# Uneven steps for the row maxima, and a new place for half a division, in a routed-attention and MLP kernel

## The chip, the cores and the metric

The kernel runs on one core of a Trainium2 chip. The metric is the device time of one execution in microseconds. Before the change it is 959.33 us, the median of three runs (959.2 to 959.88).

## What is computed

Two blocks in a row. The first is attention with routing: every query and key of a head goes to the nearest of 16 centroids, and a query sees only keys with its own centroid. The second is an MLP with its own activation.

```python
q_assign = np.argmax(einsum('bhsd,hcd->bhsc', q_n, c_n), axis=-1)   # k_assign likewise
mask = q_assign[:, :, :, None] == k_assign[:, :, None, :]
scores = np.where(mask, scale * q @ k.T, -1e9)
scores = scores - np.max(scores, axis=-1, keepdims=True)
attn = np.exp(scores); attn /= attn.sum(-1, keepdims=True) + 1e-9
x = (attn @ v) laid out as (B*S, H*D)
h = x @ w_in; g = h * erf(softplus(h)); out = g @ w_out
```

B = 4, H = 8, S = 768 keys, D = 64; the MLP has 3072 tokens, 512 and 2048 wide. All in float32.

## The kernel before

**Pairs and periods.** Two heads make a pair; there are 16 pairs. A pair has 12 units: two halves of 384 queries by six blocks of 128 keys. `period(p, i)` (from line 1345) does two units, u and u + 1, and there are six periods, i = 0 to 5, in a pair. All calls to the engines are recorded in program order (`InOrder`, line 130), so the order in which `period` calls its helpers is the order in each engine's queue. That is why every line of the profile is L138; instructions are told apart by the tiles that they write and read.

**TensorE in a period.** In this order: the first maxima step (`step_ahead`, lines 1332 and 1360); the score products of two units (`products`, f32, `sc<-qT,kT` or `sc<-more_out`); the first half of the second maxima step; the routing mask and shift of unit u (`scores`, bf16, `sc<-qm,km`), the second half of the maxima step, and `scores` of u + 1; then for the two units of the period before the product of the exponentials with v (`attend`, `turned<-pr,in_v`). After a half is complete (i = 0 and 3), `divide` (line 575) makes the denominators on TensorE (`turned<-more_out,minus`) in one bank `turned`, while the products for that half stand in the other.

**Row maxima** (`maxima_step`, line 463). The softmax's shift is made ahead, in bf16, for the pair half a pair later. For each of six blocks t of 128 queries, two steps cover the 768 keys, 384 each. A step has two passes for each of the two heads: products with the bf16 copies (`wide<-kv,qv`) and, on top, the mask (`wide<-km,qm`). VectorE then reduces both heads' 384 columns to one maximum for a row (`nmx<-wide`, 128 x 768 elements in all). `wide` is one tile of two banks of 512 columns, so no step can begin before the reduce of the one before has read it. Step number i of `maxima_step` gives t and half by `divmod(i, 2)`; in period i of a pair t = (i + 3) mod 6, the first step of the period is half 0 and the second is half 1. The second is called with `behind=True`: its mask pass uses only rows 32 to 63 and 96 to 127 of the array, and stands between the two `scores`, which use rows 0 to 31 and 64 to 95. In the first step the mask pass uses all rows and stands alone. After three blocks of t a small reduce makes `lowest`, which `turn` (line 494) brings into rows at the start of periods 0 and 3.

**Routing** (`choose`, line 407), for the pair after the next: VectorE transposes the similarities (`sims<-turned`), takes each token's maximum over 16 centroids (here written into spare columns of a score bank, `sc<-sims`), compares (`hot<-sims,sc`), and transposes twice (`aside`, `hotT`). It is a generator; `next(routing[0])` in `period` places one operation after the other. `masks` (line 437) multiplies the result by a matrix of picks (`turned<-hotT,pick`), at the places in a period that the table `MASKS` (line 50) gives: (period, place) to tensor and half. The place 0 is ahead of the products, 1 behind them, 2 behind the second `scores`. A mask above place 1 uses 32 rows for a head (`narrow`), at place 0 or 1 it uses 64.

**Division** (`divide`), a generator as well: after ScalarE's `inv`, VectorE makes `den`, divides the two halves of the products in place (`turned<-turned,inv`, twice), and writes their product with `den` to `more_out`, from where four DMAs on SP's queue store it to `x_dram`. It runs in the period after it was created, so in periods 1 and 4.

**Weights.** Beside this, the MLP's weights are loaded and brought into another form by ScalarE (`size`, `rest`, `sign`), VectorE (`bounded`, `shifted`: two tensor_scalars on 128 x 512) and GpSimd (`summed`), one block in periods 3 and 4 and one over 3, 5, 0 and 1 (lines 1400 to 1437). GpSimd also adds up the exponentials (`accumulate`).

The tail of `period` that fixes VectorE's order around the change, lines 1413 to 1418:

```python
        if i == 3:
            next(routing[0], None)
            if early(n1):
                shifted(n1)
            for _ in range(2):
                next(routing[0], None)
```

Of the kernel before, what the change touches and what calls it, by code (L numbers as in the profile page):

```python
# [14 lines left out]
ALU = mybir.AluOpType  # L15
ACT = mybir.ActivationFunctionType
AX = mybir.AxisListType
PSUM = bass.MemoryType.PSUM

P = 128  # L20
B, H, S, D = 4, 8, 768, 64
# [4 lines left out]
HW = S // 2  # L26
QW = HW // 2
TW = QW + 1
HJ = NJ // 2
HP = H // 2  # L30
NPAIR = B * HP
DM, DFF = H * D, 2048
NFT = DFF // P
# [13 lines left out]
N_LATE = 4  # L47
PLACE_OF = [n % 5 for n in range(25)] + [2, 3, 2]
LAST_X = 11
MASKS = {(0, 2): ("k", 0), (2, 0): ("q", 0), (2, 2): ("k", 1), (5, 2): ("q", 1)}  # L50
FIRST_MASKS = {(2, 0): ("k", 0), (2, 1): ("q", 0), (2, 2): ("k", 1), (5, 2): ("q", 1)}

KAPPA = {1: (0, 1), 2: (0, 0), 0: (1, 1), 3: (1, 0)}
# [93 lines left out]
def kernel(  # L147
# [24 lines left out]
    turned = [ps.tile([P, 512], F32, name=f"turned{i}") for i in range(2)]  # L172
# [149 lines left out]
    def bounded(n):  # L322
        w = w_steps[n][0]
        ve.tensor_scalar(out=w, in0=w, scalar1=2.0, scalar2=None, op0=ALU.max)
# [5 lines left out]
    def shifted(n):  # L330
        w = w_steps[n][0].bitcast(U32)
        ve.tensor_scalar(out=w, in0=w, scalar1=3, scalar2=None, op0=ALU.logical_shift_left)
# [130 lines left out]
    def maxima_step(p, i, sm=wide, behind=False):  # L463

        st = pairs[p]
        nmx = maxima[p % 2]
        t, half = divmod(i, 2)

        def passes(a, b, start, rows):
            for e in range(2):  # L470
                r = slice(e * D + rows.start, e * D + rows.stop)
                te.matmul(
                    sm[:, e, 0:HW], lhsT=st[a][r, t * P : (t + 1) * P],
                    rhs=st[b][r, half * HW : (half + 1) * HW], start=start, stop=not start,
                )

        passes("qv", "kv", True, slice(0, D))
        if behind:
            yield
        passes("qm", "km", False, slice(Q, D) if behind else slice(0, D))  # L480
        if behind:
            yield
        ve.tensor_reduce(
            out=nmx[:, :, t, half], in_=sm[:, :, 0:HW], axis=AX.X, op=ALU.max, negate=True
        )
        if i in (NJ - 1, 2 * NJ - 1):
            h = i // NJ
            ve.tensor_reduce(
                out=lowest[h][:, :, ::D].rearrange("p t e -> p e t"),
                in_=nmx[:, :, h * HJ : (h + 1) * HJ], axis=AX.X, op=ALU.min,  # L490
            )
            turns.append((p, h))
# [21 lines left out]
    def products(u):  # L514
        p, half, j = units[u]
        if u in sc_of:
            return
        st = pairs[p]
        sc = sc_of[u] = ps_s.tile([P, 2, 512], F32, name="sc", tag="s")
        for e in range(2):  # L520
            r = slice(e * D, (e + 1) * D)
            te.matmul(
                sc[:, e, 0:HW], lhsT=st["kT"][r, j * P : (j + 1) * P],
                rhs=st["qT"][r, half * HW : (half + 1) * HW], start=True, stop=False,
            )
# [49 lines left out]
    def divide(u):  # L575

        p, half, _ = units[u]
        st = pairs[p]
        av = st["av", half]

        psum = turned[1 - half][:, 0:QW]
        for g in range(4):
            te.matmul(psum[g * Q : (g + 1) * Q], lhsT=minus, rhs=st["acc", half][:, g], start=True, stop=True)

        if u + 1 < len(units):
            inv = routep.tile([P, QW], F32, name="inv")
            den = routep.tile([P, QW], F32, name="den")
        else:
            inv, den = part_of(0, 4 * HW, QW), part_of(1, 0, QW)
        ae.activation(out=inv, in_=psum, func=ACT.Ln, bias=alleps, scale=-1.0)  # L590
        ae.activation(out=inv, in_=inv, func=ACT.Exp, scale=-1.0)
        yield
        ve.scalar_tensor_tensor(
            out=den, in0=psum, scalar=S * EPS, in1=inv, op0=ALU.subtract, op1=ALU.mult
        )
        for k in range(2):
            raw = av[:, k, 0:QW]
            ve.scalar_tensor_tensor(
                out=raw, in0=raw, scalar=av[:, k, QW : QW + 1], in1=inv, op0=ALU.add, op1=ALU.mult
            )  # L600
        yield
        x = part_of(0, (2 * p + half) % 4 * HW, HW).rearrange("p (k x) -> p k x", k=2)
        ve.scalar_tensor_tensor(
            out=x, in0=den.unsqueeze(1).to_broadcast([P, 2, QW]), scalar=2.0, in1=av[:, :, 0:QW],
            op0=ALU.add, op1=ALU.mult,
        )
        b, r = divmod(p, HP)
        for g in range(4):
            rows_of, at = r * P + g // 2 * D, b * S + half * HW + g % 2 * QW
            nc.sync.dma_start(  # L610
                out=x_dram[rows_of : rows_of + D, at : at + QW].rearrange("(k r) x -> r k x", k=2),
                in_=x[g * Q : (g + 1) * Q],
            )
        if half == 1:
            del pairs[p]
        yield
# [728 lines left out]
    def period(p, i):  # L1345
        u = 2 * NJ * p + 2 * i
        n1, n2 = 2 * p - 1, 2 * p
        early = lambda n: 0 <= n < N_EARLY

        def mask(place):  # L1350
            which = (MASKS if p else FIRST_MASKS).get((i, place))
            if which:
                return masks(p + 1, *which, turned[0 if i in (0, 5) else 1], place > 1, ve if i == 0 else ae)
            return lambda: None

        if u > 0:
            for which in turns if i in (0, 3) else ():
                turn(*which)
                turns.remove(which)
            step_ahead(u)  # L1360
        mask(0)()
        next(part[0], None)
        if i == 5:
            next(routing[0], None)
        if i == 0 and p:
            run(routing[0])
        if u == 2:
            next(routing[0])
        products(u)
        products(u + 1)  # L1370
        mask(1)()
        second = step_ahead(u + 1, True) if u > 0 else iter(())
        next(second, None)
        rows = D if u == 0 or u + NJ >= len(units) else Q
        scores(u, rows)
        next(second, None)
        if i:
            next(second, None)
        next(part[0], None)
        scores(u + 1, rows)  # L1380
        later = mask(2)
        if i == 0:
            later()
            later = lambda: None
            next(second, None)
        if i == 3:
            similarities(p + 2)
            routing[0] = choose(p + 2, sc_of[u + 1][:, 0], True)
        curve(u)
        later()  # L1390
        curve(u + 1)
        if u == 0:
            step_ahead(1)
            similarities(1)
            routing[0] = choose(1, turned[0])
            next(routing[0])
            next(routing[0])
            vectors(1, "q")
            vectors(1, "k")
        if i == 0 and early(n1 - 1):  # L1400
            bounded(n1 - 1)
            shifted(n1 - 1)
            sign(n1 - 1)
        elif i == 1 and early(n1):
            size_and_rest(n1)
        elif i == 3 and early(n1):
            bounded(n1)
            sign(n1)
        elif i == 5 and early(n2):
            rest(n2)  # L1410
        for _ in range(min(len(forms), FORMS.get(p, {}).get(i, 0))):
            forms.pop(0)[0]()
        if i == 3:
            next(routing[0], None)
            if early(n1):
                shifted(n1)
            for _ in range(2):
                next(routing[0], None)
        elif i == 1:
            load(p + 1, "v", v, vp)  # L1420
            if p == 0:
                run(routing[0])
                transposes(2, "q")
        elif i == 2:
            transposes(p + 2, "k")
        elif i == 4:
            vectors(p + 2, "k")
            vectors(p + 2, "q")
        elif i == 5:
            transposes(p + 3, "q")  # L1430
        if u > 0:
            if i in POOL_FORMS.get(p, ()) and forms:
                forms.pop(0)[1]()
            if i == 1 and early(n1 - 1):
                summed(n1 - 1)
            elif i == 4 and early(n1):
                summed(n1)
            for w in (u - 2, u - 1):
                accumulate(w)
            for w in (u - 2, u - 1):  # L1440
                attend(w)
            if i % HJ == 0:
                part[0] = divide(u - 1)
                next(part[0])
        if i == 3 and early(n2):
            size(n2)
# [206 lines left out]
```

## Time and profile before

| | us |
|---|---|
| median of 3 runs | 959.33 |
| the profiled execution | 959.94 |
| its span, first to last instruction | 958.1 |
| maxima steps in the trace, first to last reduce | 12.9 to 396.1 |

| engine | share of the span busy |
|---|---|
| TensorE, matmuls | 99% |
| TensorE, weight loads | 76% |
| VectorE | 83% |
| ScalarE | 56% |
| GpSimd | 56% |

A row of the timeline gives the start, the time from the first start to the last end, engine, line, operation, output and inputs, shape, and how many instructions are merged in it; in brackets stands how long the engine sat idle before, and who ended that. Matmuls overlap: the recorded duration of one is longer than the time until the next can start, so it is the differences of starts that tell what one costs. f32 matmuls are recorded twice each. Two row-tiled matmuls, one for each head, start 3 ns apart and run side by side.

### The profile page before, as it was taken

How to read it: one execution, taken by the hardware profiler on the slowest of the kernel's cores; microseconds unless marked ns; L12 is line 12 of the kernel's file. 1: busy time of each engine (PE TensorE's matmuls, PEld its weight loads, DVE VectorE, ACT ScalarE, POOL GpSimd, SP SyncE). 2: the span in 40 equal slices, each digit the busy share in tenths (PEclk: the TensorE clock that was granted, in tenths of full speed). 3: DMA queues.
4: the chain of work that ended last, by engine and by line, in shares of the span. 5: the costliest groups of instructions: out<-in, count | busy, mean ns of one | idle time of the engine just before them, and what ended most of it. 6: DMA issues, size and time to landing. Idle time of an engine off the chain costs nothing.

```text
span 958.1 us, 22447 instructions
## 1 busy us (share of the span) xinstructions
PE 950.1 (99%) x8954; PEld 728.2 (76%) x8954; DVE 798.0 (83%) x1395; ACT 539.0 (56%) x815; POOL 538.7 (56%) x375
## 2 busy tenths in 40 slices
PE   8999999999999999999999999999999999999998
PEld 3555555555555555588888888998999899989987
DVE  8888888888888887787689889788868987897887
ACT  3777777777777777542524531654257236625541
POOL 1688888778888888897669910360054016202600
PEclk9999999999999999999999999999999999999999
DMA  9345545544454522041403454463445336343533
GB/s 224 61 112 112 112 111 112 112 112 111 90 117 84 132 56 56 22 152 55 177 1 154 154 164 138 135 202 110 155 125 174 115 128 210 110 149 119 157 115 110
DMA packets 172313, 116.06 MB, mean 121 GB/s; under 512 B 131376, under 2 KB 141104, under 8 KB 172208
## 3 DMA queue, kind: packets, MB, share of 16 engines
q1 hardware_dynamic: 169280, 113.41, 42.3%
q8 instruction: 71, 1.16, 0.5%
q10 hardware_dynamic: 2928, 1.21, 0.4%
q14 instruction: 34, 0.28, 0.1%
HBM read 90.21 MB, written 24.38 MB: 120 GB/s over the span
## 4 chain that ended last, share of the span: by engine, by line
PE 95%; DVE 2%; ACT 1%; DMA 1%; issue 0%; DVEq 0%; SPq 0%; ACTq 0%
PE bank L138 41%; PE turned L138 32%; PE sc L138 17%; PE wide L138 6%; DVE nmx L138 1%; DMA out_dram<-osb 0%; ACT a_s L138 0%; DVE osb L138 0%; ACT L138 0%; DVE g L138 0%; DMA in_q<-in_q_dram 0%; DVE g_more L138 0%; DVE kT L138 0%; DVE sims L138 0%; DVE qT L138 0%
## 5 line engine op out<-in xcount | busy, mean ns | idle before, releaser
L138 POOL TENSOR_TENSOR more_out<-more_out,pr 128x768 f32<-128x768 f32 x128 | 217.3, 1698 | 16.2 <-ACT pr L138 6.7
L138 DVE TENSOR_REDUCE nmx<-wide 128x2 f32<-128x768 f32 x189 | 180.5, 955 | 46.4 <-PE wide L138 45.9
L138 ACT ACTIVATE pr<-sc 128x768 f32<-128x768 f32 x192 | 148.7, 810 | 87.2 <-PE wide L138 68.6
L138 POOL TENSOR_TENSOR g<-g 128x512 f32<-128x512 f32 x36 | 47.2, 1310 | 216.6 <-DVE g L138 214.7
L138 PE MATMUL turned<-pr,in_v 128*32 128x193 f32 x3072 | 144.8, 330 | 0.0
L138 PEld LDWEIGHTS turned<-pr,in_v 128*32 128x32 f32 x3072 | 91.5, 109 | 50.7 <-issue 21.3
L138 PE MATMUL sc<-qT,kT 64*128 64x384 f32 x528 | 98.3, 486 | 0.0
L138 DVE TENSOR_TENSOR g<-g 128x512 f32<-128x512 f32 x114 | 79.0, 693 | 15.2 <-PE bank L138 11.7
L138 DVE TENSOR_TENSOR g<-a_s,g 128x512 f32<-128x512 f32 x80 | 73.5, 944 | 5.6 <-ACT a_s L138 5.6
L138 DVE TENSOR_TENSOR g<-bank,g 128x256 f32<-128x256 f32 (+1 forms) x129 | 63.8, 522 | 15.3 <-PE bank L138 8.1
L138 PE MATMUL bank<-w_out,g 128*128 128x256 f32 x328 | 75.4, 379 | 0.0
L138 ACT ACTIVATE a_s<-g 128x1024 f32<-128x1024 f32 (+1 forms) x36 | 41.0, 1149 | 55.9 <-POOL g L138 45.3
L138 PE MATMUL bank<-g_more,g 128*128 128x256 f32 x304 | 71.8, 379 | 0.0
L138 PE MATMUL bank<-x_own,w_in 128*128 128x128 f32 (+1 forms) x432 | 71.6, 308 | 0.0
L138 POOL TENSOR_TENSOR more_out<-pr,pr 128x768 f32<-128x768 f32 x32 | 58.9, 1839 | 20.1 <-ACT pr L138 20.1
L138 PEld LDWEIGHTS bank<-w_out,g 128*128 128x128 f32 x328 | 62.3, 190 | 8.5
L138 PEld LDWEIGHTS <-qv 64*128 64x128 bf16 x384 | 26.9, 93 | 53.4 <-issue 37.3
L138 PEld LDWEIGHTS sc<-qT,kT 64*128 64x128 f32 x528 | 49.2, 187 | 21.9 <-ACT inv L138 3.1
L138 ACT ACT_TABLE_LOAD x40 | 51.3, 1283 | 24.4 <-DVE g L138 23.7
L138 PE MATMUL wide<-kv,qv 64*128 64x384 bf16 x378 | 63.9, 328 | 1.1 <-ACT km L138 0.6
L138 PEld LDWEIGHTS bank<-x_own,w_in 128*128 128x128 f32 x432 | 61.1, 191 | 4.0 <-issue 0.6
L138 PEld LDWEIGHTS bank<-g_more,g 128*128 128x128 f32 x304 | 57.8, 190 | 7.9
(242 smaller groups left out, 2065.3 us busy)
## 6 DMA issues: line engine op xcount, KB each, us to landing
g_more<-b_dram SPq DMA_DIRECT2D x48, 512.0 KB, 3.5
g_more<-w_dram SPq DMA_DIRECT2D x84, 256.0 KB, 2.8
x_own<-in_moe_w_in_dram SPq DMA_DIRECT2D x13, 512.0 KB, 5.4
in_v<-in_v_dram SPq DMA_DIRECT2D x32, 192.0 KB, 3.3
x_dram<-more_out SPq DMA_DIRECT2D x128, 48.0 KB, 1.7
x_own<-x_dram SPq DMA_DIRECT2D x6, 1024.0 KB, 5.4
in_k<-in_k_dram SPq DMA_DIRECT2D x59, 96.0 KB, 2.7
in_q<-in_q_dram SPq DMA_DIRECT2D x58, 96.0 KB, 4.9
```

The source lines that it names most:

```text
L138: ins = getattr(self.engine, name)(*args, **kw)
```

## The change

The split of the 768 keys between the two steps now depends on the block t: 256 + 512 for t = 0, 1 and 4, 352 + 416 for t = 2 and 5, 384 + 384 for t = 3. In VectorE's queue, `hot` moves from the end of period 3 behind the first reduce of period 4; `bounded` moves behind the transpose of the similarities; of the division only `den` and the first half stay ahead of the second reduce of the period, the second half and the product go behind it. The maxima over the centroids are written to spare columns of `turned[0]` in place of a score bank. One mask in period 2 moves from ahead of the products to a new place 3, between the products of u and of u + 1, still 64 rows wide.

```diff
+KEYS = (256, 256, 352, 384, 256, 352)
...
-MASKS = {(0, 2): ("k", 0), (2, 0): ("q", 0), (2, 2): ("k", 1), (5, 2): ("q", 1)}
+MASKS = {(0, 2): ("k", 0), (2, 3): ("q", 0), (2, 2): ("k", 1), (5, 2): ("q", 1)}
...
         t, half = divmod(i, 2)
+        first = KEYS[t]
+        keys = (slice(0, first), slice(first, S))[half]
+        n = keys.stop - keys.start
...
-                    sm[:, e, 0:HW], lhsT=st[a][r, t * P : (t + 1) * P],
-                    rhs=st[b][r, half * HW : (half + 1) * HW], start=start, stop=not start,
+                    sm[:, e, 0:n], lhsT=st[a][r, t * P : (t + 1) * P],
+                    rhs=st[b][r, keys], start=start, stop=not start,
...
-            out=nmx[:, :, t, half], in_=sm[:, :, 0:HW], axis=AX.X, op=ALU.max, negate=True
+            out=nmx[:, :, t, half], in_=sm[:, :, 0:n], axis=AX.X, op=ALU.max, negate=True
...
             ve.scalar_tensor_tensor(
                 out=raw, in0=raw, scalar=av[:, k, QW : QW + 1], in1=inv, op0=ALU.add, op1=ALU.mult
             )
-        yield
+            if k == 0:
+                yield
...
-                return masks(p + 1, *which, turned[0 if i in (0, 5) else 1], place > 1, ve if i == 0 else ae)
+                return masks(p + 1, *which, turned[0 if i in (0, 5) else 1], place == 2, ve if i == 0 else ae)
...
         mask(0)()
+        if i == 4:
+            next(routing[0], None)
         next(part[0], None)
...
         products(u)
+        mask(3)()
         products(u + 1)
...
         if i:
             next(second, None)
-        next(part[0], None)
+            next(part[0], None)
         scores(u + 1, rows)
...
             next(second, None)
+            next(part[0], None)
         if i == 3:
             similarities(p + 2)
-            routing[0] = choose(p + 2, sc_of[u + 1][:, 0], True)
+            routing[0] = choose(p + 2, turned[0], True)
...
         elif i == 3 and early(n1):
-            bounded(n1)
             sign(n1)
...
             next(routing[0], None)
             if early(n1):
+                bounded(n1)
                 shifted(n1)
-            for _ in range(2):
-                next(routing[0], None)
...
                 attend(w)
+            if i == 3:
+                next(routing[0], None)
             if i % HJ == 0:
                 part[0] = divide(u - 1)
```

In the build VectorE's rows from period 3 to 5 then stand as: `sims`, `bounded`, `shifted`, the maxima (`turned<-sims`), first reduce, `hot`, `den`, first half of the division, second reduce, second half, product. Before they are: `bounded`, `sims`, `shifted`, the maxima (`sc<-sims`), `hot`, first reduce, `den`, both halves, second reduce, product.

## The prediction

> **What bounds the kernel now.** I read the page's first lines, then a window over the stretch that the change touches.
>
> ```profile
> span 958.1 us, 22447 instructions
> PE 950.1 (99%) x8954; PEld 728.2 (76%) x8954; DVE 798.0 (83%) x1395; ACT 539.0 (56%) x815; POOL 538.7 (56%) x375
> ...
> 24.00:396.00 372.00, 371.94 (x5356) 212.10 (x5359) 313.66 (x504) 284.98 (x462) 305.77 (x188) 1.00 0.43 97
> ```
>
> The third line covers the time in which row maxima are made (columns: window, length, busy of PE, PEld, DVE, ACT, POOL, granted clock, DMA share). TensorE is busy for all of it at full clock, so only what shortens TensorE's own row of starts counts. But "busy" is a sum of modelled durations that overlap; a small wait hides in it. So next I read the timeline for the starts alone: first the tail of a period i = 3 and the whole of i = 4 on TensorE.
>
> ```profile
> 201.94 1.45 PE L138 MATMUL sc<-qT,kT 64*128 64x384 f32 x8
> 203.23 0.33 PE L138 MATMUL wide<-kv,qv 64*128 64x384 bf16 x2
> 203.49 0.34 PE L138 MATMUL sc<-qm,km 32*128 32x384 bf16 x2
> 203.50 0.34 PE L138 MATMUL wide<-km,qm 32*128 32x384 bf16 x2
> 203.66 0.32 PE L138 MATMUL sc<-qm,km 32*128 32x384 bf16 x2
> ...
> 205.89 0.51 PE L138 MATMUL turned<-more_out,minus 128*32 128x192 f32 x8
> 206.34 0.34 PE L138 MATMUL wide<-kv,qv 64*128 64x384 bf16 x2
> 206.51 0.33 PE L138 MATMUL wide<-km,qm 64*128 64x384 bf16 x2
> 206.67 1.48 PE L138 MATMUL sc<-qT,kT 64*128 64x384 f32 x8
> 208.01 0.34 PE L138 MATMUL wide<-kv,qv 64*128 64x384 bf16 x2
> 208.28 0.34 PE L138 MATMUL sc<-qm,km 32*128 32x384 bf16 x2
> 208.29 0.33 PE L138 MATMUL wide<-km,qm 32*128 32x384 bf16 x2
> ...
> 210.16 0.34 PE L138 MATMUL wide<-kv,qv 64*128 64x384 bf16 x2
> ```
>
> A period has two maxima steps. The first (206.34, 206.51) runs alone: each 384-column pass holds TensorE for 0.16 to 0.17 us. The second has its qv pass alone (203.23) and its qm pass (203.50) between the two score passes (203.49, 203.66), on rows that these leave free, so that one costs TensorE nothing.
>
> The block of score products takes 1.29 us where nothing disturbs it (201.94 to 203.23), but 1.34 in period 4 (206.67 to 208.01), and the pass behind it 0.27 instead of 0.26. That is a wait of 0.06 us. Who causes it stands in VectorE's rows of the same time:
>
> ```profile
> 203.93 0.96 DVE L138 TENSOR_REDUCE nmx<-wide 128x2 f32<-128x768 f32 x1 [0.83 <-PE wide L138]
> 204.81 0.43 DVE L138 TENSOR_SCALAR w_in<-w_in 128x512 f32<-128x512 f32 x1
> 205.16 0.57 DVE L138 STREAM_TRANSPOSE sims<-turned 128x384 f32<-128x384 f32 x1
> 205.66 0.38 DVE L138 TENSOR_SCALAR w_in<-w_in 128x512 uint32<-128x512 uint32 x1
> 205.96 0.54 DVE L138 TENSOR_REDUCE sc<-sims 128x24 f32<-128x384 f32 x1
> 206.54 0.55 DVE L138 TENSOR_TENSOR hot<-sims,sc 128x384 bf16<-128x384 f32 x1
> 207.01 0.95 DVE L138 TENSOR_REDUCE nmx<-wide 128x2 f32<-128x768 f32 x1
> 207.87 0.35 DVE L138 SCALAR_TENSOR_TENSOR den<-turned,inv 128x192 f32<-128x192 f32 x1
> 208.14 0.89 DVE L138 SCALAR_TENSOR_TENSOR turned<-turned,inv 128x192 f32<-128x192 f32 x2
> 208.94 0.95 DVE L138 TENSOR_REDUCE nmx<-wide 128x2 f32<-128x768 f32 x1
> 209.80 0.54 DVE L138 SCALAR_TENSOR_TENSOR more_out<-den,turned 128x384 f32<-128x384 f32 x1
> ```
>
> The reduce of the first step starts at 207.01, behind the routing's comparison (`hot`), and ends at 207.96; the second step's first pass, which overwrites `wide`, starts at 208.01. So there is a release time of 0.05 us and VectorE's queue is what ends last there, by 0.06 us a pair. Period 1 has the same wait, from two tensor_scalars ahead of its reduce; its products block in the first and in the last of 14 pairs:
>
> ```profile
> 47.43 1.45 PE L138 MATMUL sc<-qT,kT 64*128 64x384 f32 x8
> 48.73 0.34 PE L138 MATMUL wide<-kv,qv 64*128 64x384 bf16 x2
> ...
> 365.62 1.45 PE L138 MATMUL sc<-more_out 64*128 64x384 f32 x8
> 366.98 0.34 PE L138 MATMUL wide<-kv,qv 64*128 64x384 bf16 x2
> ```
>
> 1.30 and 1.36 us, so waits of 0.02 to 0.08 with the pass behind; I take 0.05.
>
> **The change part by part.** *KEYS.* In periods 1, 3 and 4 (t = 4, 0, 1) the first step takes 256 keys and the second 512; in 2 and 5 it is 352 and 416; in period 0 nothing changes. The two qv passes run alone in both steps, and their columns still add up to 768: no change. The first step's qm pass runs alone and shrinks; the second step's qm pass grows, but beside the scores: 0.16 us x 512/384 = 0.21 us is under the 0.33 us of two score passes. So each 256/512 period saves what 128 columns cost: 0.16/384 x 128 = 0.053 us, if the weight load behind it stays hidden. Its nearest rows are in the second half of the kernel:
>
> ```profile
> L138 PEld LDWEIGHTS bank<-x_own,w_in 128*128 128x128 f32 x432 | 61.1, 191 | 4.0 <-issue 0.6
> ...
> 599.28 1.05 PE L138 MATMUL turned<-x_own,w_in 128*128 128x128 f32 x8
> 600.17 1.06 PE L138 MATMUL bank<-x_own,w_in 128*128 128x128 f32 x8
> ```
>
> Eight f32 matmuls of 128 columns, each with its own weight load, recorded at 191 ns, follow one another in 0.89 us, 0.111 each. A recorded load of 191 ns is thus no floor, and a 256-column bf16 pass can take 0.111. I take 0.16 - 0.11 = 0.05; bounds 0 and 0.053. Number: t = 0 and 1 in 15 pairs each (made ahead in periods 3 and 4), t = 4 in 16: 46 x 0.05 = **2.3 us**. The 352 steps save 0.16/384 x 32 = 0.013 us each, 31 times, less up to 0.006 where the routing mask behind the scores then waits for the 416-column pass: **0.2 us** (0 to 0.4).
>
> The Trainium skill, page "TensorE: Matmul & The Clock Gate", section "Back-to-back issue gap", gives for a sustained stream 81 ns a matmul at 128 columns and 131 at 512, about 0.13 ns a column, and speaks against this cut. By that the cut would be worth some 0.017 us, 0.8 us in all. The trace has 0.16 us for 384 columns and 0.11 for 128 f32 ones and doesn't agree.
>
> *VectorE's order.* Period 4: the reduce of the first step now stands ahead of `hot` and is 256 elements shorter. The reduce rows above give the price: 0.54 us for 384 elements, 0.96 for 768, so 1.09 ns an element: 0.68 for 2 x 256, 1.24 for 2 x 512. The routing's maxima, 0.3 us later behind the long reduce of period 3, end at about 206.8 (205.96 + 0.54 + 0.3); the reduce then ends at 207.5, and TensorE comes for `wide` at 207.9. The wait goes: 13 pairs x 0.06 = **0.8 us**. In period 1 the reduce ends 0.28 us earlier, and the wait goes too: 14 x 0.05 = **0.7 us**.
>
> What is late next? (a) The long reduce of the second step. At 203.50 to 203.93 a reduce starts 0.43 us after its pass; with 512 columns 0.48; it ends at 0.48 + 1.24 = 1.72, releases at 1.77, and the next period's pass is due 1.87 us after (208.29 to 210.16): 0.10 us to spare, because half the division now stands behind it. (b) In period 3 the routing's transpose must leave `turned` before the denominators (205.89, 2.39 us after 203.50). `bounded` now stands behind it, so it starts at 1.63, ends at 2.20, releases at 2.25. (c) The second half of the division and the output product follow that reduce: 1.72 + 0.36 + 0.45 = 2.53, that is 0.66 us into the next period instead of 0.18 (209.80 + 0.54 against 210.16). In period 5 the first reduce starts behind them, 0.06 late, and is 64 elements or 0.07 us shorter. In period 2 the mask into the same bank, now between the two product blocks, comes at 0.16 + 0.15 + 0.64 = 0.95. In its old place, at 0.31, it would wait. The mask itself costs what it costs now:
>
> ```profile
> 222.33 0.32 PE L138 MATMUL turned<-hotT,pick 64*128 64x384 bf16 x1
> 222.34 1.61 PE L138 MATMUL sc<-more_out 64*128 64x384 f32 x8
> 223.70 0.41 PE L138 MATMUL wide<-kv,qv 64*128 64x384 bf16 x2
> 224.04 0.33 PE L138 MATMUL sc<-qm,km 32*128 32x384 bf16 x2
> ```
>
> 1.36 + 0.34 instead of 1.29 + 0.26: 0.15 us, one lone pass on half the rows, at either place. (d) `bounded` and `shifted` end at about 206.4 instead of 206.04; GpSimd's sum waits for both, but for ScalarE longer:
>
> ```profile
> 206.80 1.29 POOL L138 TENSOR_TENSOR w_in<-w_in,x_own 128x512 int32<-128x512 int32 x1 [1.84 <-ACT x_own L138]
> ```
>
> So it costs nothing with 0.4 us of cover. (e) The maxima of the similarities go to the spare columns of `turned`, so `hot`, now late, no longer holds a score bank; the price of the reduce stays. No DMA changes place: SP's queue, and the output stores behind the product, move with (c) and are needed long after.
>
> **Sum.** 2.3 + 0.2 + 0.8 + 0.7 = 4.0 us less; some 0.1 may be lost in the last pair, where GpSimd's sums end shortly before TensorE needs them. The profiled execution took 959.94 us (span 958.1), so 956.0; it lay 0.6 above the median of the runs shown. From the median, 959.33 - 3.9 = **955.4 us**. The stages behind follow TensorE and shift with it.
>
> **Rivals.** *The short pass does not shrink* (a fixed cost of a pass or of the weight load behind it): the 2.3 and the 0.2 are lost, 957.8 us. For it: no 256-column bf16 pass stands between f32 weights in the trace; against it: the 0.111 us above. By the skill's figures it would be 957.1. Chance 0.10.
>
> *The waits stay* because TensorE's 0.06 is not VectorE's: the change then doesn't do the half it says; 959.33 - 2.4 = 956.9. Against it: the ends and starts 0.05 us apart. Chance 0.05.
>
> *VectorE becomes the bound:* if the long reduce costs as much per element as the short routing reduce, 0.54/384 x 1024 = 1.44 us, margin (a) is overdrawn by 0.10 in 31 periods and (b) by 0.06 in 15: 4.0 us back, 959.4. It decides from 1.34 us on. Against it: the 0.96 of 768 elements, which lies far under proportion. Chance 0.11, spread from 956 to 959.4.
>
> *TensorE's row groups wait for one another* (slower): if the second score pass cannot start beside a longer pass still running, but waits for its end and for the 0.10 us that a change of row groups costs (203.23 to 203.49, less the pass's 0.16), it starts 0.31 instead of 0.17 us after the first: 46 x 0.14 = 6.5 us, 961.8; with the 416-column passes as well 31 x 0.11 more, 965.3. It decides from 3.9/46 = 0.085 us a period. For it: now all four passes are equally long, so the trace has no such case. Against it: at 222.33 one half of the rows carries the mask while the other begins the products 0.01 us later, and the halves run on unequal without a stop. Chance 0.07.
>
> **How the numbers follow.** The forecast, 954.6 to 956.4, has 0.65; 0.02 is for better than that. Range 953.9 to 958.6: it takes in the first two rivals and the lower part of the third; some 0.06 of VectorE's case and the 0.07 of the row groups stay above, 0.02 below. A measurement of this kernel tells about 0.2% from no change, 1.9 us: faster is below 957.4. That is the forecast and better (0.67), the waits staying (0.05), 0.03 of the short pass and 0.05 of VectorE's case: 0.80. Same: 0.07 and 0.06, 0.13. Slower: 0.07.
>
> **What would show it.** Right: the first step's qm pass to the products 0.11 instead of 0.16 us in periods 1, 3, 4; the second score pass still 0.17 after the first; products blocks of 1.29 in periods 1 and 4; the reduces at 0.68 and 1.24; a pair 24.15 instead of 24.43 us long. Wrong: a pass at 0.16; new gaps ahead of `wide` in periods 2 and 5, of the denominators in 3, or of the moved mask.

## The result, and the profile after

Ten executions of the changed kernel have a median of 957.14 us (955.71 to 957.43), ten of the kernel before 959.61 (959.2 to 959.88): ratio 0.9974, 95% interval 0.9964 to 0.9984. That is 2.5 us less, where 3.9 were forecast. The profiled execution took 955.71 us and is the lowest of its ten; the other nine lie between 956.99 and 957.43 us. So the trace shows a gain of 4.2 us (span 958.1 to 953.9) which most executions don't have. Where the 1.4 us between them go is the main question of the experiments.

The page's first lines of the changed kernel:

```profile
span 953.9 us, 22420 instructions
## 1 busy us (share of the span) xinstructions
PE 945.8 (99%) x8954; PEld 723.1 (76%) x8954; DVE 796.9 (84%) x1395; ACT 540.8 (57%) x815; POOL 538.4 (56%) x375
```

TensorE is the bound as before, busy for 4.3 us less. Its timeline in the changed kernel, from the denominators of period 3 to period 5:

```profile
204.15 0.51 PE L139 MATMUL turned<-more_out,minus 128*32 128x192 f32 x8
204.59 0.28 PE L139 MATMUL wide<-kv,qv 64*128 64x256 bf16 x2
204.71 0.27 PE L139 MATMUL wide<-km,qm 64*128 64x256 bf16 x2
204.82 1.46 PE L139 MATMUL sc<-qT,kT 64*128 64x384 f32 x8
206.11 0.38 PE L139 MATMUL wide<-kv,qv 64*128 64x512 bf16 x2
206.43 0.34 PE L139 MATMUL sc<-qm,km 32*128 32x384 bf16 x2
206.43 0.39 PE L139 MATMUL wide<-km,qm 32*128 32x512 bf16 x2
206.60 0.32 PE L139 MATMUL sc<-qm,km 32*128 32x384 bf16 x2
...
208.30 0.32 PE L139 MATMUL wide<-kv,qv 64*128 64x352 bf16 x2
```

Read the differences of starts. The lone mask pass holds TensorE for 0.11 us (204.71 to 204.82) instead of 0.16. The products block takes 1.29 (204.82 to 206.11) instead of 1.34. The second score pass still starts 0.17 after the first (206.43 to 206.60), although a 512-column pass runs beside them. From the denominators to period 5 it is 4.15 us (204.15 to 208.30) instead of 4.27 (205.89 to 210.16).

VectorE in the same time:

```profile
202.20 1.23 DVE L139 TENSOR_REDUCE nmx<-wide 128x2 f32<-128x1024 f32 x1 [1.12 <-PE wide L139]
203.34 0.57 DVE L139 STREAM_TRANSPOSE sims<-turned 128x384 f32<-128x384 f32 x1
203.83 0.85 DVE L139 TENSOR_SCALAR w_in<-w_in 128x512 f32<-128x512 f32 x2
204.59 0.56 DVE L139 TENSOR_REDUCE turned<-sims 128x24 f32<-128x384 f32 x1
205.06 0.68 DVE L139 TENSOR_REDUCE nmx<-wide 128x2 f32<-128x512 f32 x1
205.66 0.55 DVE L139 TENSOR_TENSOR hot<-sims,turned 128x384 bf16<-128x384 f32 x1
206.12 0.35 DVE L139 SCALAR_TENSOR_TENSOR den<-turned,inv 128x192 f32<-128x192 f32 x1
206.38 0.42 DVE L139 SCALAR_TENSOR_TENSOR turned<-turned,inv 128x192 f32<-128x192 f32 x1
206.86 1.23 DVE L139 TENSOR_REDUCE nmx<-wide 128x2 f32<-128x1024 f32 x1
208.00 0.42 DVE L139 SCALAR_TENSOR_TENSOR turned<-turned,inv 128x192 f32<-128x192 f32 x1
```

The reduces take 0.68 and 1.23 us, as computed. The short one ends at 205.74, 0.37 us before TensorE comes for `wide`; the long one at 208.09, 0.21 before. Over the patterned pairs 1 to 14, half pairs of periods 3 to 5 go from 12.46-12.48 to 12.31 us (two of the thirteen took 0.12 and 0.18 us longer before, one 0.06 after), those of periods 0 to 2 from 11.96-12.04 to 11.88-11.92. At the end of the attention TensorE's starts are 3.97 us earlier than before, where 4.0 were forecast; how the two come to agree stands further down. The MLP behind it is where executions part.

### The profile page after: what moved, and what is told of

It reads as the page before. It is cut to its first block, busy times and chain, and to the rows that moved or that the text cites. A ratio compares the mean times of both kernels' runs of the same rounds, so it can differ in the third digit from the quotient of the medians.

```text
span 953.9 us, 22420 instructions
## 1 busy us (share of the span) xinstructions
PE 945.8 (99%) x8954; PEld 723.1 (76%) x8954; DVE 796.9 (84%) x1395; ACT 540.8 (57%) x815; POOL 538.4 (56%) x375
## 4 chain that ended last, share of the span: by engine, by line
PE 96%; DVE 1%; ACT 1%; issue 0%; DMA 0%; SPq 0%; DVEq 0%; ACTq 0%
PE bank L139 42%; PE turned L139 32%; PE sc L139 17%; PE wide L139 6%; DVE nmx L139 0%; ACT a_s L139 0%; DMA in_k<-in_k_dram 0%; ACT L139 0%; DVE g L139 0%; SPq L139 0%; DVE kT L139 0%; DVE osb L139 0%; DVE g_more L139 0%; DVE sims L139 0%; ACT km L139 0%
## 5 line engine op out<-in xcount | busy, mean ns | idle before, releaser
L139 DVE TENSOR_REDUCE nmx<-wide 128x2 f32<-128x1024 f32 (+2 forms) x189 | 179.5, 950 | 40.2 <-PE wide L139 39.2
L139 PE MATMUL wide<-kv,qv 64*128 64x512 bf16 (+2 forms) x378 | 64.9, 327 | 1.0 <-ACT km L139 0.6
L139 PE MATMUL wide<-km,qm 32*128 32x512 bf16 (+2 forms) x378 | 62.4, 326 | 0.0
```

Of the source, the lines that this page charges most:

```text
L139: ins = getattr(self.engine, name)(*args, **kw)
```

## The experiments

Where a run tests the change itself (2 to 4 and 7 to 11), theory A is the prediction: TensorE gains by the shorter lone passes and by two waits, and each move in VectorE's order is needed because a queue there ends last. Runs 1, 5 and 6 ask where the 1.4 us go. Ratios are to the kernel before in the same session.

**1. The changed kernel again, unaltered.**

> The changed kernel once more, unaltered, for a second trace and more times: nine of its ten executions took 957.0 to 957.4 us, the profiled one 955.7. Theory A (the 1.4 us are in the attention stage, where a margin of VectorE is overdrawn in most executions): a trace of a slower execution has pairs longer than the 24.19 us of the first trace, by about 0.1 us each. Theory B (they are outside it, in the start or in the MLP, where a transfer or a table load ends later): the pairs are 24.19 us long again and the difference stands in one or two places. Time by both 955.7 to 957.4, mostly 957.1.

Measured: 957.17 us (955.67 to 958.12), ratio 0.9971 (0.9961 to 0.9981); the profiled execution took 957.13. B holds as to the place: its attention is as long as in the first trace, and against that one it loses 0.9 us at 443 to 445 us and 0.4 at 469 to 471, in the start of the MLP. At that place the timeline of this run has VectorE's rows

```profile
417.04 0.42 DVE L139 TENSOR_TENSOR g<-bank,g 128x256 f32<-128x256 f32 x1
417.43 1.53 DVE L139 TENSOR_SCALAR w_out<-w_out 128x512 f32<-128x512 f32 x1
418.88 1.27 DVE L139 TENSOR_TENSOR g<-bank,g 128x256 f32<-128x256 f32 x3
420.07 1.57 DVE L139 TENSOR_SCALAR w_out<-w_out 128x512 uint32<-128x512 uint32 x1
```

and GpSimd's

```profile
417.40 1.28 POOL L139 TENSOR_TENSOR a_s<-w_in 128x512 f32<-128x512 f32 x1
418.76 1.34 POOL L139 TENSOR_TENSOR x_own<-w_in,a_s 128x512 f32<-128x512 f32 x1
420.07 1.29 POOL L139 TENSOR_TENSOR w_out<-w_out,g_more 128x512 int32<-128x512 int32 x1
```

while the kernel before has, in the same order of engines,

```profile
421.23 0.41 DVE L138 TENSOR_SCALAR w_out<-w_out 128x512 f32<-128x512 f32 x1
```

```profile
421.25 1.53 POOL L138 TENSOR_TENSOR a_s<-w_in 128x512 f32<-128x512 f32 x1
```

The same two instructions meet in both. Before, VectorE starts 0.02 us ahead: it takes 0.41, and GpSimd 1.53 instead of 1.28. Here GpSimd starts 0.03 us ahead: it takes 1.28, and VectorE 1.53 instead of 0.41. Whichever is first holds the other up. That costs VectorE 1.1 us or GpSimd 0.25. It comes again at 420.07, with 1.57.

VectorE itself makes this up: by 430 us it again waits for TensorE, and so 0.13 us behind the first trace, as TensorE is. GpSimd doesn't. Its next three instructions on `w_out` start 0.13 or 0.14 us after VectorE's tensor_scalars on it end, the third 1.6 us later than in the first trace, and it stays that late. The first trace has only GpSimd's last instruction of this block beside VectorE's next two:

```profile
435.74 1.26 POOL L139 TENSOR_TENSOR more_out<-more_out,w_out 128x512 f32<-128x512 f32 x1
436.32 1.83 DVE L139 TENSOR_TENSOR g<-a_s,g 128x512 f32<-128x512 f32 x2 [1.34 <-ACT a_s L139]
```

This run has the last two beside them; the later one is shown:

```profile
436.50 3.07 DVE L139 TENSOR_TENSOR g<-a_s,g 128x512 f32<-128x512 f32 x2 [1.41 <-ACT a_s L139]
437.30 1.72 POOL L139 TENSOR_TENSOR more_out<-more_out,w_out 128x512 f32<-128x512 f32 x1
```

The two VectorE instructions take 3.07 us instead of 1.83. From there VectorE is 1.3 us late, and TensorE waits for it, in this run's timeline,

```profile
443.25 1.10 PE L139 MATMUL bank<-x_more,more_in 128*128 128x256 f32 x4
444.78 1.10 PE L139 MATMUL turned<-x_own,w_in 128*128 128x256 f32 x4 [0.43 <-DVE g L139]
```

1.53 us from start to start. In the first trace of the changed kernel it is 0.87:

```profile
442.98 1.03 PE L139 MATMUL bank<-x_more,more_in 128*128 128x256 f32 x4
443.85 1.03 PE L139 MATMUL turned<-x_own,w_in 128*128 128x256 f32 x4
```

The Trainium skill, page "SBUF — State Buffer", section "Who interferes with whom", states this rule: VectorE and GpSimd share a port pair that a tensor_scalar in a two-port mode takes as an exclusive lock, and whoever issues first blocks the other for the whole instruction. The trace agrees to within 0.14 us: 0.41 became 1.53 beside a GpSimd instruction of 1.28, where waiting for its whole end would give 1.66, while VectorE's three `g<-bank,g` at 418.88, with one operand in PSUM, took 1.27 beside GpSimd as they do elsewhere.

**2. The steps alone, in the old order.** The kernel before with `KEYS` and nothing else.

```diff
+KEYS = (256, 256, 352, 384, 256, 352)
...
-                    rhs=st[b][r, half * HW : (half + 1) * HW], start=start, stop=not start,
+                    rhs=st[b][r, keys], start=start, stop=not start,
```

> The kernel before with uneven steps alone, VectorE's order as it was. Theory A (the new order is what makes room for the long reduce): the lone mask pass shrinks to 0.11 us as in the changed kernel (2.4 us less), but the transposed similarities come behind the long reduce and a tensor_scalar, 0.2 us after the denominators are due, and the second reduce of period 4 stands behind the whole division, 0.2 us too late for period 5: 13 pairs x 0.4 us lost, in all 961 to 963 us. Theory B (uneven steps carry the gain, the order is a detail): 957.0 to 957.5 us.

Measured: 966.33 us (965.9 to 968.51), ratio 1.0075 (1.0062 to 1.0088). A in kind, but 4 us more than it computed: the order is worth 9.2 us to these steps, and without it they lose. (In the attention alone it is 10.4 us; the trace of this run has VectorE first in the MLP, most executions of the changed kernel do not.) In the trace each pair is 0.76 us longer than in the changed kernel: 0.26 at the denominators of period 3, 0.13 at `wide` in period 4, 0.23 ahead of period 2, 0.16 at the mask in period 2. The term that A lacked stands in VectorE's waits over the attention:

```profile
DVE den L139 <- ACT inv L139: 4.4, 15, 0.5
```

In period 1 `den` waits 0.3 us a pair for ScalarE's reciprocal, and with the whole division ahead of the second reduce everything behind it waits too. (In the changed kernel `den` waits there too, 0.28 us in the first seven pairs and 0.1 in the others, but only half of the division stands between it and the reduce.)

**3. The order alone.** The changed kernel with even steps.

```diff
-KEYS = (256, 256, 352, 384, 256, 352)
+KEYS = (384, 384, 384, 384, 384, 384)
```

> The changed kernel with 384 + 384 keys in all blocks, so with the new order alone. Theory A (order removes the wait of period 4 alone; that of period 1 goes only with the shorter reduce): products blocks of 1.29 us in period 4 and of 1.30 to 1.37 in period 1 as before; 0.8 us less than before, 958.8 us. Theory B (the order removes both waits): 958.1 us. Theory C (the uneven steps carry nothing): 957.1 us.

Measured: 960.47 us (959.6 to 960.89), ratio 1.0009 (1.0 to 1.0017). All three expectations missed. The trace has the two reasons. The wait of period 4 is gone (products block 1.339 to 1.290 us), but the one of period 1 is not: 1.30 in the first seven pairs, 1.40 to 1.42 in the others. There the order puts nothing else ahead; only a shorter reduce helps. So the attention, from its first denominators to its last, is just 0.5 us shorter than before (in this trace it ends 0.2 us earlier, because it began 0.3 later). And the MLP loses 1.3 us between 447 and 474 us by the same meeting of VectorE and GpSimd, GpSimd first, which no theory had. Without that loss the time would be about 959.2, near A's 958.8.

**4. The mask at its old place.**

```diff
-MASKS = {(0, 2): ("k", 0), (2, 3): ("q", 0), (2, 2): ("k", 1), (5, 2): ("q", 1)}
+MASKS = {(0, 2): ("k", 0), (2, 0): ("q", 0), (2, 2): ("k", 1), (5, 2): ("q", 1)}
```

> The changed kernel with the mask of period 2 in its old place, ahead of the products. Theory A (the product of the division now ends 0.66 us into period 2, 0.3 us after the mask's old place): TensorE waits about 0.35 us ahead of that mask in 14 pairs, 5 us, 962 us. Theory B (there is room enough, and a lone mask costs the same at both places): no difference from the changed kernel, 957.1 us.

Measured: 963.57 us (962.5 to 963.68), ratio 1.004 (1.0025 to 1.0054). A, 1.6 us above its 962: the start of the mask moves from 0.16 to 0.61 us behind the pass ahead of it, 0.455 us a pair or 6.4 us. At the new place the changed kernel shows no wait in front of it:

```profile
220.37 0.81 PE L139 MATMUL sc<-more_out 64*128 64x384 f32 x4
221.01 0.32 PE L139 MATMUL turned<-hotT,pick 64*128 64x384 bf16 x1
221.01 0.96 PE L139 MATMUL sc<-more_out 64*128 64x384 f32 x4
221.66 0.49 PE L139 MATMUL wide<-kv,qv 64*128 64x416 bf16 x2
```

**5. GpSimd a little later.** If the 1.4 us are decided by who starts first, one tiny GpSimd instruction must give them back in every execution.

```diff
-        for _ in range(MADE_BEFORE[n - N_EARLY]):
+        for made in range(MADE_BEFORE[n - N_EARLY]):
+            if made == 1:
+                t = up.tile([P, HM], F32, name="u")
+                ge.tensor_tensor(out=t[:, 0:1], in0=minus[:, 0:1], in1=minus[:, 0:1], op=ALU.add)
```

> The changed kernel with one small GpSimd instruction more (one column, two operands) at the start of the MLP, ahead of the second of the three forms that GpSimd makes for the latest weights. In the first trace of the changed kernel VectorE's tensor_scalar on w_out ran before GpSimd's addition into a_s, and the span was 953.9 us; in the second GpSimd's addition came 36 ns earlier than VectorE's instruction, both took two to three times as long, and the span was 955.3. Theory A (the two executions differ in which of these two goes first): GpSimd now always goes second, so the median falls from 957.15 us to 955.5-956.0. Theory B (the later executions lose 1.3 us for another reason, a late transfer say): 957.0-957.3, as without the instruction.

Measured: 956.03 us (955.76 to 956.21), ratio 0.9962 (0.9949 to 0.9974). Theory A: no execution is near 957. The timeline of this run, VectorE,

```profile
417.66 0.44 DVE L139 TENSOR_SCALAR w_out<-w_out 128x512 f32<-128x512 f32 x1
418.02 1.27 DVE L139 TENSOR_TENSOR g<-bank,g 128x256 f32<-128x256 f32 x3
419.20 0.42 DVE L139 TENSOR_SCALAR w_out<-w_out 128x512 uint32<-128x512 uint32 x1
```

and GpSimd,

```profile
417.62 0.20 POOL L139 TENSOR_TENSOR u<-minus 128x1 f32<-128x1 f32 x1
417.76 1.48 POOL L139 TENSOR_TENSOR a_s<-w_in 128x512 f32<-128x512 f32 x1
```

The added instruction takes 0.20 us and GpSimd's long one follows at 417.76, after VectorE has begun. Theory B is out as well: ScalarE waits 3.3 us here for the weight transfer ahead of this place, as in run 1 (3.4; the first trace of the changed kernel has 3.0), so the transfer is late and the loss still gone. One instruction more makes the kernel 1.1 us faster. This is the fastest of all versions.

**6. The control: the same instruction in the kernel before.** The edit is that of run 5.

> The kernel before with the same small GpSimd instruction. In its trace VectorE's tensor_scalar on w_out already goes first (at 6.583 us behind the last denominators matmul, GpSimd's addition at 6.603). Theory A: nothing left to gain, 959.4-959.9 us against 959.6 without it. Rival (the instruction speeds the start of the MLP whichever goes first): 958.0-958.6, and then the gain of the other run is no evidence for A.

Measured: 959.73 us (959.58 to 960.29), ratio 1.0002 (0.9993 to 1.0011). Theory A: nothing to gain where VectorE is first already.

**7. The whole division ahead of the second reduce.**

```diff
-            if k == 0:
-                yield
+        yield
```

> The changed kernel with both divisions ahead of the second reduce of a half pair again, only the product behind it. Theory A (the run with the uneven steps alone lost 0.23 us ahead of the denominators of period 1 because the denominator waited for ScalarE and held up the second reduce; 0.15 us in period 4): 14 x 0.23 + 14 x 0.15 = 5.3 us more than 957.15, so 962.0-962.8. Theory B (the reduce has margin enough, and the loss of that run came from the routing's order alone): 957.0-957.5.

Measured: 962.38 us (961.14 to 962.86), ratio 1.0026 (1.0016 to 1.0036). Theory A in size: the product with v of period 1 takes 1.677 instead of 1.447 us until TensorE goes on, that of period 4 1.594; 0.23 and 0.147 a pair, 5.3 us over 14 pairs.

**8. The comparison ahead of the first reduce of period 4.**

```diff
         mask(0)()
-        if i == 4:
-            next(routing[0], None)
...
             if i == 3:
                 next(routing[0], None)
+                next(routing[0], None)
```

> The changed kernel with the routing's comparison (hot, 0.46 us) ahead of the first reduce of period 4 again. The first reduce then ends 0.47 us later and its first score pass waits for it. Theory A (margin of the first reduce about 0.33 us): 0.14 us x 14 pairs = 2 us more than 957.15, so 958.8-959.5. Theory B (the shorter first reduce of 2 x 256 columns pays for the comparison): 957.0-957.4.

Measured: 960.82 us (959.73 to 961.1), ratio 1.001 (1.0001 to 1.0019): A, and 1.7 us more than its 2. VectorE in this run:

```profile
206.71 0.56 DVE L139 TENSOR_REDUCE turned<-sims 128x24 f32<-128x384 f32 x1
207.30 0.55 DVE L139 TENSOR_TENSOR hot<-sims,turned 128x384 bf16<-128x384 f32 x1
207.77 0.69 DVE L139 TENSOR_REDUCE nmx<-wide 128x2 f32<-128x512 f32 x1
```

From the maxima to the reduce it is 1.06 us instead of 0.47: the comparison costs 0.59, not its 0.46, because it also waits until the maxima that it reads are written. Behind an independent reduce that wait is free. TensorE loses 0.28 a pair; 0.59 - 0.28 = 0.31 is the margin of the short reduce (0.37 in the rows of the changed kernel, less the release).

Runs 9 to 12 start from the kernel of run 5, so that the meeting in the MLP doesn't blur them; their reference is 956.03 us.

**9. One tensor_scalar ahead of the similarity transpose again.**

```diff
         elif i == 3 and early(n1):
+            bounded(n1)
             sign(n1)
...
             if early(n1):
-                bounded(n1)
                 shifted(n1)
```

> The changed kernel with the small GpSimd instruction at the start of the MLP (956.03 us), and the first of the two tensor_scalars of period 3 put ahead of the similarity transpose again, as before the change. Theory A (the long reduce of 2 x 512 in period 3 ends at the limit of what the transpose can wait for): the transpose leaves turned 0.43 us later, about 0.13 to 0.20 us past the moment at which the denominators need it, x 13 pairs = 1.7 to 2.6 us, so 957.7-958.7. Theory B (the transpose has margin and only the comparison had to move): 955.8-956.3.

Measured: 959.19 us (958.75 to 959.38), ratio 0.9993 (0.9984 to 1.0002): A, 0.5 us above its range. The denominators of period 3 start 0.24 us later and stall 0.02 more, 0.26 a pair. So of the tensor_scalar's 0.43 us there was a margin for 0.17.

**10. The last even step made uneven too.**

```diff
-KEYS = (256, 256, 352, 384, 256, 352)
+KEYS = (256, 256, 352, 256, 256, 352)
```

> The same 956.03 us kernel with the last even step (period 0, 384 and 384 keys) made 256 and 512 as well, so in all four sixths. Theory A (VectorE's order sets where the short step can be): TensorE gains 0.107 - 0.053 = 0.05 us a pair in the passes, but the second reduce of period 0 stands behind the additive mask's tensor_scalar and becomes 0.28 us longer with some 0.10 us of margin, and the reduce of period 1 behind it is late too: 0.28 us of waits in all; net 0.23 x 14 = 3.2 us, so 958.3-959.7. Theory B (a short step gains wherever it is): 14 x 0.05 = 0.7 us less, 955.1-955.5.

Measured: 959.0 us (958.62 to 959.54), ratio 0.9993 (0.9984 to 1.0001). A. The 0.21 us a pair stand between the denominators and period 1 (0.652 instead of 0.441 us), where TensorE waits for the long reduce. The passes gain nothing: the 0.107 us of the first step go in equal parts to the 512-column qv pass (0.053) and to the mask behind the scores (0.053 later), which uses the rows of the long mask pass.

**11. The steps of 352 at 256.**

```diff
-KEYS = (256, 256, 352, 384, 256, 352)
+KEYS = (256, 256, 256, 384, 256, 256)
```

> The same 956.03 us kernel with the two steps of 352 and 416 keys (periods 2 and 5) at 256 and 512. Theory A (the minimum over the row maxima stands behind the long reduce, and the turning matmuls that need it begin within 0.1 us of its end): the reduce is 0.20 us longer, all of it a wait, x 28 = 5.6 us, less 28 x 0.04 = 1.1 us of shorter passes, so 960.0-961.0. Theory B (margin there): 954.9-955.2.

Measured: 959.75 us (959.23 to 961.04), ratio 1.0002 (0.9993 to 1.0011). A in kind, 0.25 us under its range: the turning matmuls start 0.12 us later in each half pair, and here too the masks behind the scores take what the passes give (0.04 us).

**12. Room for the last uneven step.**

```diff
-KEYS = (256, 256, 352, 384, 256, 352)
+KEYS = (256, 256, 352, 256, 256, 352)
...
-                return masks(p + 1, *which, turned[0 if i in (0, 5) else 1], place == 2, ve if i == 0 else ae)
+                return masks(p + 1, *which, turned[0 if i in (0, 5) else 1], place == 2)
...
         if i == 0:
-            later()
-            later = lambda: None
             next(second, None)
...
             shifted(n1 - 1)
-            sign(n1 - 1)
...
-            if i == 1 and early(n1 - 1):
-                summed(n1 - 1)
-            elif i == 4 and early(n1):
+            if i == 4 and early(n1):
...
                 accumulate(w)
+            if i == 2 and early(n1 - 1):
+                summed(n1 - 1)
...
                 next(part[0])
+            if i == 0 and early(n1 - 1):
+                sign(n1 - 1)
```

> The last even step at 256 and 512 keys as in the run before last, and room made for it: the additive mask of period 0 is formed by ScalarE behind the first exponential instead of by VectorE ahead of the second reduce, the sign of that weight step moves behind the two ScalarE steps of the division, and its GpSimd sum behind the additions of period 2. Theory A: 0.05 x 14 = 0.7 us and the 0.1 us left in period 1 of the late pairs come free, so 955.0-955.5. Rival (ScalarE or GpSimd becomes late: the mask holds up the second exponential by 0.4 us, the sum the additions of period 2): 0.1 to 0.3 us a pair, 957-960.

Measured: 967.31 us (967.26 to 967.95), ratio 1.0081 (1.0067 to 1.0094). A falls, and what the rival named isn't the cause either. The first pairs lose 0.10 us each, the last seven 1.49. The timeline of such a pair, VectorE,

```profile
215.68 1.23 DVE L139 TENSOR_REDUCE nmx<-wide 128x2 f32<-128x1024 f32 x1 [0.64 <-PE wide L139]
216.82 3.04 DVE L139 TENSOR_SCALAR w_in<-w_in 128x512 f32<-128x512 f32 x2
219.78 0.68 DVE L139 TENSOR_REDUCE nmx<-wide 128x2 f32<-128x512 f32 x1
```

GpSimd,

```profile
216.33 1.28 POOL L139 TENSOR_TENSOR more_in<-w_in 128x512 f32<-128x512 f32 x1
217.75 1.82 POOL L139 TENSOR_TENSOR more_out<-pr,pr 128x768 f32<-128x768 f32 x1
```

and TensorE:

```profile
220.51 0.39 PE L139 MATMUL wide<-kv,qv 64*128 64x512 bf16 x2 [1.24 <-DVE nmx L139]
```

The two tensor_scalars that take 0.85 us alone take 3.04. Each falls into a GpSimd instruction that began before it, and the reduce behind them keeps TensorE waiting. It is the meeting of run 1 at another place. In run 5 the addition that here starts at 217.75 stands behind the sum that was moved, and starts at 218.95. So freeing one queue sent another engine's work into it. The run makes three moves at once, and which of them matter beside this one was not separated. The 0.10 us of the first pairs lie in period 0 (4.187 instead of 4.089 us) and were not followed further.

## Why the prediction was right, and which step failed

The kernel is faster, as forecast, and the time lies inside the range; it is 1.7 us above the 955.4 forecast, and above the 954.6 to 956.4 that had most of the chance.

*The short lone pass:* right. 0.163 us became 0.109, and 0.173 of the qv pass 0.119, which the 512-column pass takes back (0.258 to 0.311). With 0.003 us more in the products block that is 0.050 a period, 46 x 0.050 = 2.3 us. The rival that passes don't shrink is out. (The prediction also took its 0.11 from eight f32 rows 0.111 us apart. As f32 matmuls are recorded twice, those are four matmuls, and that the two figures meet is chance; the share of the columns, 0.16/384 x 256, is what the trace bears out.) The Trainium skill's formula for a single matmul in "TensorE: Matmul & The Clock Gate", section "Back-to-back issue gap", columns / 2.4 + 2.5 ns, gives 109, 149, 162 ns for 256, 352, 384 columns; the trace has 0.109, 0.149, 0.162 us. Its sustained figures, weighed in the prediction, don't hold for these passes: 128 columns more cost a qv pass 0.053 us, where the estimate from them gives 0.017.

*The 352 steps:* forecast 0.2 us, measured under 0.1. The prediction allowed 0.006 us for the mask behind the scores; it waits 0.012 to 0.013 longer and takes back all of what the pass gives.

*The waits:* period 4 gave its 0.06 x 13 = 0.8 us. Period 1 gave 0.025 us in the first seven of these pairs and some 0.04 in the last seven, 0.4 to 0.5 us rather than 0.7: the products block there still takes 1.30 to 1.32 in most late pairs. Run 3 shows that it is the shorter reduce that works in period 1, runs 3 and 8 that it is the order in period 4.

*The sum over the attention:* 4.0 us forecast, 3.97 in the trace, and that they lie so close is in part luck. The four terms came to 2.3, under 0.1, 0.8 and 0.5, some 3.6 us. Another 0.24 us is single waits that the prediction didn't name: the kernel before takes 4.91 and 4.85 us instead of 4.73 for the periods 3 at 250.6 and 324.2 us (run 6's trace has both as well), the changed kernel 4.74 instead of 4.68 for one at 175.7. Most of the rest is a start that came 0.08 us earlier in this trace. A pair takes 24.18 us in the first half of the attention, where the prediction had 24.15.

*The margins:* (a) and (d) held. (b) was put at 0.14 us, and run 9 measures 0.17. (c) was right in kind: the mask at its old place costs 0.455 us a pair (run 4), where its 0.66 less 0.31 gives 0.35. The prediction didn't see that splitting the division is needed for a further reason, ScalarE's late reciprocal in period 1: there the whole division costs 0.23 us a pair, in period 4, where `den` doesn't wait, 0.147 (run 7).

*The row groups:* the second score pass follows 0.173 us after the first beside a 512-column pass, as it did beside one of 384, so that rival is out. *VectorE as the bound* is out at 1.23 us against the 1.34 from which it decides, though runs 7 to 11 show how near it is: each of them costs 3 to 5 us.

*The step that failed* is the last sentence of the sum: "The stages behind follow TensorE and shift with it." They follow TensorE, but VectorE and GpSimd meet at the start of the MLP within some 0.04 us of each other, and in most executions of the changed kernel, to judge by their times, GpSimd goes first, which costs 1.3 us. Run 5 shows the cost: with GpSimd put later, the gain is 3.6 us at the median (959.68 to 956.03), no execution is slower than 956.21, and that is close to the 3.9 forecast. The fourteen traces agree: VectorE's tensor_scalar takes 1.53 or 1.54 us in the five in which GpSimd's addition starts first (runs 1, 3, 4, 7 and 8), and 0.41 to 0.86 in the nine others. What shifts the two engines by those hundredths is not settled. Run 3, with the order alone, has GpSimd first, run 2, with the steps alone, has VectorE first; neither edit touches the instructions concerned. In the profiled execution of the changed kernel VectorE was 0.53 us ahead (416.91 against 417.44). There ScalarE had waited 0.32 us less for a weight transfer, and VectorE's next instructions followed ScalarE; that this alone made the lead was not tested.

## What to carry to other kernels

Cut the columns of a matmul that runs alone and give them to one that runs beside others, but look at what follows on the same rows: a mask there takes the gain back in the three periods that have one. An uneven split lengthens a reduce, so find each queue behind it first; here the order of VectorE's instructions decided between 2.5 us won and 6.7 lost by the same split. And before trusting a difference of a microsecond, look for two engines that start within hundredths of each other and hold each other up: move one of them on purpose.

## What the runs showed of the hardware

- A VectorE tensor_scalar of 128 x 512 f32 (0.41 us) and a GpSimd addition of the same size (1.28) all but exclude each other. The later one took 1.53 us whichever it was: VectorE ended 0.28 us after GpSimd (run 1), GpSimd 1.14 after VectorE (the kernel before). A lead of 0.01 us (run 2) to 0.04 was enough to decide. Two such tensor_scalars took 3.04 instead of 0.85 (run 12), and two VectorE `g<-a_s,g` 3.07 beside GpSimd (run 1), where the next two behind them took 1.28 with GpSimd idle.
- A bf16 pass ahead of f32 products costs 0.109 us at 256 columns, 0.149 at 352 and 0.162 at 384: in proportion, and down to 256 columns no floor shows.
- Two passes on other rows don't mind a longer one beside them (0.173 us from score pass to score pass next to 384, 416 and 512 columns), but the next pass on the long one's own rows does (0.013 us later at 416 columns in the changed kernel, 0.053 at 512 in run 10).
- VectorE's reduce took 0.65 to 0.69 us for 512 elements and 1.23 for 1024; an instruction that reads what the one before it wrote pays 0.13 us more than its place in the queue (run 8).
